# Pooled attention, two heads of a pair on the two halves of the array, in front of two MoE layers

## The chip, the cores and the metric

One Trainium2 chip, one core. The metric is the device time of one execution of the whole kernel in microseconds (us). One profiled execution gives the trace that is read here. Engines: PE is TensorE (PEld its weight loads), DVE VectorE, ACT ScalarE, POOL GpSimd, SP the engine whose queue issues the DMAs.

## What is computed

```python
def attention(q, k, v):              # 4 batches, 8 heads, 1152 keys, head size 64
    q_pool = q.reshape(B, H, S // 2, 2, D).mean(axis=3)          # 576 queries
    scores = scale * q_pool @ k.transpose(0, 1, 3, 2)
    scores = scores - max(scores, axis=-1)
    attn = exp(scores); attn = attn / (sum(attn, axis=-1) + 1e-9)
    return attn @ v
x = attention(q, k, v) as (2304, 512)
h = x @ w_in;   x = (h - tanh(h)) @ w_out            # layer 1, 512 -> 2048 -> 512
h = x @ w2_in;  out = (h * sigmoid(1.702 h)) @ w2_out
```

All in float32. The weights of the two layers come as 8-byte floats.

## The kernel before

A float32 product of full precision is made in one of two ways: as three products in fp32r of a high and a low part (hi·hi, lo·hi, hi·lo), or as one product of plain float32.

**Attention** (L212 to L727) goes over 16 pairs of heads. Keys lie on 128 partitions for two heads: the head size is 64, so one head fills half of the rows. To use all 128 rows, `stack` (L311) builds by six DMAs for each head a stationary array `a1` (high part of k over low part) and `a2` (high part of k over a row of ones), and moving arrays `q2` (high part of q twice) and `q3` (low part of q over the row of minus the maximum). `scores` (L423) makes the scores of one step, 128 keys by 576 queries of one head, in two halves of 288 queries, each from two fp32r products (L433, L434), and takes exp of them on ACT twice: into `pf` (L439) and, for two steps of three, rounded into `ph` (L449). `rest` (L452) makes `pl = pf - ph` on DVE or POOL (L457). A step later `pv` (L459) multiplies by v: for two steps of three six fp32r products (L479), for the third two float32 products (L469). The stationary side is 65 columns wide: v and a column of ones, so row 64 of the result is the sum of the exponentials. There are 18 steps in a pair, nine for each head.

The maximum of every query row is known beforehand: `max_tile` (L322) makes for the next pair a block-diagonal product (`bdqs`, L296) of 128 columns by 288 keys twice (L327) and reduces it on DVE (L331), 18 times for a pair. `max_rows` (L385) transposes the maxima on DVE (L392) and writes them as a row by four DMAs for each head (L400). The first pair has its own opening (L560 to L655): products that only keep PE at work (`keep_warm`, L617), and the maxima of head 0 on 64 rows (`first_max`, L337; L346, L353), with rows made by PE (`row_part`, L360).

A pair's end: `u` takes the result (L485), `sums` (L490) moves the sums by DMA, `recip` (L499), `merge` (L507), `spread` (L513) bring back the reciprocals and `normalise` (L521) writes `xb`.

**What sets the order.** The order of the work on every engine is written out by hand: the loop from L689 issues for each step the scores, the maxima, the rest and the product of three steps before (`LAG`, L538), and the dictionaries `plan`, `opening` and `early` say at which pair and step the preparations of the next pairs run (q sums L283, their split L290 and L294, k's split L303 and L307). `early` also loads seven of the first eight pieces of weights and converts them on DVE (L138, L144, L151, L158), ACT and POOL (L166). Each engine takes its instructions in that order. PSUM has eight banks: two score tiles of two banks, one tile of two for the maxima and two accumulators.

**The two layers** (L729 to L917) follow on the same engines; the last of the eight pieces (`last_o`) is loaded in the attention and converted in the first steps of layer 1. The first product of layer 1 is L755.

Of the kernel before, what the change touches and what calls it, by code (L numbers as in the profile page):

```python
# [7 lines left out]
F32 = mybir.dt.float32  # L8
# [20 lines left out]
def tile_pooled_attention_two_moe(  # L29
# [9 lines left out]
    first: bass.AP,  # L39
# [47 lines left out]
    KG = KT // 3  # L87
    last = 2 * NPAIR - 1
    h0, h1, h2 = last % 3, (last - 1) % 3, (last - 2) % 3
# [8 lines left out]
    a1s, vhs, vls = [{}, {}, {}]  # L98
    for i, at in ((h2, 0), (h1, 3 * S), (h0, 8 * S)):
        a1s[i] = part(at, S)  # L100
        vhs[i] = part(at + S, KT, 128)
        vls[i] = part(at + 2 * S, KT, 128)
    bdqs = [part(6 * S + i * S, S) for i in range(2)]
# [108 lines left out]
    def attention(ctx: ExitStack):  # L212
        ap = ctx.enter_context(tc.tile_pool(name="attn", bufs=1))

        stacks = []
        for i in range(3):
            a1 = a1s[i]
            a2 = ap.tile([D + 1, S], F32R, name=f"a2_{i}")
            q2 = ap.tile([128, SP], F32R, name=f"q2_{i}")
            q3 = ap.tile([D + 1, SP], F32R, name=f"q3_{i}")  # L220
            stacks.append((a1, a2, q2, q3))
        vfs = [rbd[:, SP:SP + KG * 128].rearrange("p (a b) -> p a b", a=KG)] + [
            ap.tile([128, KG, 128], F32, name=f"vf{i}") for i in range(1, 3)]
        vt = [(vhs[i], vls[i]) for i in range(3)]

        def outer(t):
            return t.rearrange("p (m r) d -> p m r d", r=3)[:, :, 0:3:2, 0:D]

        def whole(t):
            return t % 3 == 1  # L230
        nc.vector.memset(f32(bdqs[1][:, 0:128]), 0.0)
        nc.vector.memset(f32(bdqs[1][:, 128:]), 0.0)
        zeros = bdqs[1][:, 0:128], bdqs[1][:, 0:1].to_broadcast([128, 512])

        def refill_v(i, n):
            old, new = [(*vt[x], vfs[x])[n] for x in (0, i)]
            nc.scalar.activation(new[:, :, D:D + 2], old[:, :, D:D + 2], AF.Copy)

        def refill_row(i):
            row = [stacks[x][1][D:D + 1, :] for x in (0, i)]  # L240
            nc.scalar.activation(row[1], row[0], AF.Copy)

        def fill(i):
            vh, vl = vt[i]
            nc.gpsimd.memset(f32(stacks[i][1][D:D + 1, :]), 1.0)
            nc.gpsimd.memset(f32(vh[:, :, D:D + 2]), 1.0)
            nc.gpsimd.memset(f32(vl[:, :, D:D + 2]), 0.0)
            nc.gpsimd.memset(vfs[i][:, :, D:D + 2], 1.0)

        mts = []  # L250
        for i in range(2):
            mt = ap.tile([128, 32], F32R, name=f"mt{i}")
            nc.vector.memset(f32(mt[:]), 0.0)
            mts.append(mt)

        qraw, kraw, vraw, pairs = {}, {}, {}, {}

        def load_q(p, rows=slice(0, 128)):
            if p not in qraw:
                qraw[p] = ap.tile([128, 2, SP], F32, tag="qr", name="qr")  # L260
            nc.sync.dma_start(out=qraw[p][rows], in_=q[p // NPB, p % NPB][rows])

        def load_k(p, rows=slice(0, 128)):
            if p not in kraw:
                kraw[p] = ap.tile([128, S], F32, tag="kr", name="kr", bufs=2)
            nc.sync.dma_start(out=kraw[p][rows], in_=k[p // NPB, p % NPB][rows])

        def load_v(p, s):
            vraw[p, s] = ap.tile([128, 2 * KG, D], F32, tag=f"vr{s}", name=f"vr{s}")
            nc.sync.dma_start(out=vraw[p, s], in_=v[p // NPB, p % NPB][:, s, 0:2 * KG])  # L270

        def new_pair(p):
            pairs[p] = dict(
                qs=ap.tile([128, SP], F32, tag="qs", name="qs"),
                qh=ap.tile([128, SP], F32R, tag="qh", name="qh", bufs=2),
                ql=ap.tile([128, SP], F32R, tag="ql", name="ql", bufs=2),
                kh=ap.tile([128, S], F32R, tag="kh", name="kh", bufs=2),
                kl=ap.tile([128, S], F32R, tag="kl", name="kl"),
                mt=mts[p % 2],
            )  # L280

        def sum_q(p, eng=nc.vector):
            eng.tensor_add(pairs[p]["qs"], qraw[p][:, 0], qraw[p][:, 1])  # L283

        def prep_qs(p, eng=nc.vector):
            new_pair(p)
            sum_q(p, eng)

        def prep_qh(p):
            nc.scalar.activation(pairs[p]["qh"], pairs[p]["qs"], AF.Copy)  # L290

        def prep_ql(p, eng=nc.vector):
            d = pairs[p]
            eng.tensor_tensor(d["ql"], d["qs"], f32(d["qh"][:]), op=ALU.subtract)  # L294

        def prep_bdq(p, s):  # L296
            r = slice(64 * s, 64 * s + 64)
            nc.scalar.activation(
                bdqs[p % 2][r, s * SP:(s + 1) * SP], pairs[p]["qs"][r, :], AF.Copy)

        def prep_kh(p, x):
            xs = slice(x * SP, (x + 1) * SP)
            nc.scalar.activation(pairs[p]["kh"][:, xs], kraw[p][:, xs], AF.Copy)  # L303

        def prep_kl(p, x):
            xs = slice(x * SP, (x + 1) * SP)
            nc.gpsimd.tensor_tensor(  # L307
                pairs[p]["kl"][:, xs], kraw[p][:, xs], f32(pairs[p]["kh"][:, xs]),
                op=ALU.subtract)

        def stack(p, s):  # L311
            d = pairs[p]
            a1, a2, q2, q3 = stacks[(2 * p + s) % 3]
            r = slice(64 * s, 64 * s + 64)
            nc.sync.dma_start(out=f32(a1[0:64, :]), in_=f32(d["kh"][r, :]))
            nc.sync.dma_start(out=f32(q2[0:64, :]), in_=f32(d["qh"][r, :]))
            nc.sync.dma_start(out=f32(a1[64:128, :]), in_=f32(d["kl"][r, :]))
            nc.sync.dma_start(out=f32(q2[64:128, :]), in_=f32(d["qh"][r, :]))
            nc.sync.dma_start(out=f32(a2[0:64, :]), in_=f32(d["kh"][r, :]))
            nc.sync.dma_start(out=f32(q3[0:64, :]), in_=f32(d["ql"][r, :]))  # L320

        def max_tile(p, j, x=0, pool=None, parts=2, n=HB):  # L322
            d = pairs[p]
            mx = (pool or ps_mx).tile([128, parts, 512], F32, tag="mx", name="mx")
            for a in range(parts):
                k0 = (x * parts + a) * n
                nc.tensor.matmul(  # L327
                    mx[:, a, 0:n], bdqs[p % 2][:, 128 * j:128 * j + 128], d["kh"][:, k0:k0 + n],
                    start=True, stop=True)
            c = 16 * x + j  # L330
            nc.vector.tensor_reduce(  # L331
                d["mt"][:, c:c + 1], mx[:, :, 0:n], AX.XY, ALU.max, negate=True)

        ident = bdqs[0][:, 0:128]
        first_mt = bdqs[0][:, 128:288]

        def first_max(s, j, x, pool, parts, n, banks=2):  # L337
            d = pairs[0]
            a1, _, q2, _ = stacks[0]
            r = slice(64 * s, 64 * s + 64)  # L340
            lhs, rhs = (q2, a1) if s == 0 else (d["qh"], d["kh"])
            mx = pool.tile([128, banks, 512], F32, tag="mx", name="mx")
            if j < 4:
                for a in range(parts):
                    k0 = (x * parts + a) * n
                    nc.tensor.matmul(  # L346
                        mx[:, a, 0:n], lhs[r, 128 * j:128 * j + 128], rhs[r, k0:k0 + n],
                        start=True, stop=True)
            else:
                for a in range(parts):  # L350
                    for h in range(2):
                        q0, k0 = 512 + 64 * s - 64 * h, h * SP + a * n
                        nc.tensor.matmul(  # L353
                            mx[:, a, 0:n], bdqs[1][r, q0:q0 + 128], rhs[r, k0:k0 + n],
                            start=(h == 0), stop=(h == 1))
            c = 64 + 16 * x + 5 * s + j
            nc.vector.tensor_reduce(
                first_mt[:, c:c + 1], mx[:, 0:parts, 0:n], AX.XY, ALU.max, negate=True)

        def row_part(s, row, j):  # L360
            c = 5 * s + j
            nc.tensor.matmul(row, first_mt[:, c:c + D + 1], ident, start=True, stop=True)

        def first_row(s, row):
            for j in range(4):
                row_part(s, row[0:D + 1, 128 * j:128 * j + 128], j)

        def copy_row(s, row):
            nc.scalar.activation(stacks[s][3][D:D + 1, 0:512], row[D:D + 1, 0:512], AF.Copy)
# [604 lines left out]
```

## Time and profile before

| | us |
|---|---|
| median of 3 runs | 1302.81 (1298.59 to 1303.04) |
| the profiled execution, its own time | 1298.67 |
| span in its trace, first to last instruction | 1296.0 |
| start of the first product of layer 1 in it | 496.81 |
| mean granted TensorE clock | 0.999 of full |

The span is 2.7 us shorter than the execution's own time. Times in the rows further down are counted from the start of the span. A matmul's record is longer than its share of the engine, since they are pipelined; what one costs is read from the starts of its followers.

### The profile page before, as it was taken

The page shows a single profiled execution, that of the slowest core. Times are in us where ns is not written, and L with a number is a line of the kernel's source. Part 1 is how long each engine was busy: PE and PEld are TensorE (multiplying, and loading weights), DVE is VectorE, ACT ScalarE, POOL GpSimd, SP SyncE. Part 2 cuts the span into 40 slices and gives each one's busy share as a digit, 9 for nine tenths or more (in the row PEclk, how much of TensorE's full clock was granted, in tenths as well). Part 3 has the DMA queues.
Part 4 walks back from the last instruction along what each step waited for, and adds up shares of the span by engine and source line. Part 5 has one row for each costly group of instructions (what it writes and reads, how often), then busy time and mean ns, then how long its engine had stood idle before and what let it go on. Part 6 is the DMA issues. An engine that isn't in the chain of part 4 may idle for free.

```text
span 1296.0 us, 18915 instructions
## 1 busy us (share of the span) xinstructions
PE 1284.7 (99%) x7043; PEld 1134.3 (88%) x7043; DVE 986.5 (76%) x1277; ACT 752.2 (58%) x1159; POOL 358.7 (28%) x277
## 2 busy tenths in 40 slices
PE   9999999999999999999999999999999999999998
PEld 6899999999999988889889889889888889889887
DVE  6787887887978888999999999999944645645433
ACT  6777777777777777786666666666543323222211
POOL 7533333333333332233333333332101100100000
PEclk9999999999999999999999999999999999999999
DMA  7777666676667630211111111111211101111012
GB/s 205 177 176 172 170 157 160 170 184 169 170 168 172 145 96 18 74 33 52 51 40 39 49 33 50 33 33 50 80 34 33 52 30 50 49 33 33 25 41 81
DMA packets 58739, 116.25 MB, mean 90 GB/s; under 512 B 24856, under 2 KB 28952, under 8 KB 58648
## 3 DMA queue, kind: packets, MB, share of 16 engines
q1 hardware_dynamic: 58648, 115.05, 34.1%
q8 instruction: 55, 0.90, 0.3%
q14 instruction: 36, 0.29, 0.1%
HBM read 66.58 MB, written 4.79 MB: 55 GB/s over the span
## 4 chain that ended last, share of the span: by engine, by line
PE 77%; DVE 13%; ACT 6%; issue 2%; POOL 1%; DVEq 0%; POOLq 0%; ACTq 0%
PE y L850 21%; PE h L755 20%; PE pv L479 11%; PE pv L469 7%; PE mx L327 6%; PE sc L434 6%; PE sc L433 6%; DVE gg L813 2%; DVE gg L796 2%; ACT u L794 2%; DVE wt L144 1%; ACT a L815 1%; DVE wt L138 1%; DVE xb L870 1%; DVE wt L151 1%
## 5 line engine op out<-in xcount | busy, mean ns | idle before, releaser
L331 DVE TENSOR_REDUCE mt<-mx 128x1 fp32r<-128x576 f32 x270 | 203.7, 754 | 82.0 <-PE mx L327 76.5
L439 ACT ACTIVATE pf<-sc 128x576 f32<-128x576 f32 x288 | 187.4, 652 | 122.8 <-PE sc L434 112.4
L755 PE MATMUL h<-hl,big 128*128 128x512 f32 (+1 forms) x940 | 211.6, 377 | 0.0
L755 PEld LDWEIGHTS h<-hl,big 128*128 128x128 f32 x940 | 174.0, 188 | 28.5
L850 PE MATMUL y<-g,big 128*128 128x512 f32 (+1 forms) x780 | 185.3, 368 | 1.5 <-POOL g L767 1.5
L433 PE MATMUL sc<-q,big 128*128 128x288 f32 x576 | 182.6, 331 | 0.1
L850 PE MATMUL y<-big,g 128*128 128x512 f32 x702 | 181.0, 390 | 0.0
L166 POOL TENSOR_TENSOR big<-wt,big 128x512 fp32r<-128x512 f32 x46 | 61.3, 1332 | 379.7 <-ACT big L165 379.7
L434 PE MATMUL sc<-q,a 65*128 65x288 f32 x576 | 162.8, 297 | 0.0
L850 PEld LDWEIGHTS y<-g,big 128*128 128x128 f32 x780 | 142.7, 188 | 21.4 <-POOL g L767 3.1
L765 ACT ACTIVATE g<-gg 128x1024 fp32r<-128x1024 f32 (+1 forms) x80 | 78.0, 974 | 138.5 <-DVE gg L826 76.3
L850 PEld LDWEIGHTS y<-big,g 128*128 128x128 f32 x702 | 131.7, 188 | 27.1
L479 PE MATMUL pv<-ph,big 128*65 128x288 f32 x768 | 141.6, 295 | 0.5 <-ACT u L485 0.5
L870 DVE TENSOR_TENSOR xb<-xb,y 128x512 f32<-128x512 f32 (+1 forms) x114 | 72.2, 656 | 86.8 <-PE y L850 86.8
L457 DVE TENSOR_TENSOR pl<-pf,ph 128x576 fp32r<-128x576 f32 x159 | 133.7, 841 | 2.2 <-ACT ph L449 1.5
L755 PE MATMUL h<-hl,w 128*128 128x512 f32 (+1 forms) x564 | 127.0, 377 | 0.0
L449 ACT ACTIVATE ph<-sc 128x576 fp32r<-128x576 f32 x188 | 121.9, 649 | 0.0
L755 PEld LDWEIGHTS h<-hl,w 128*128 128x128 f32 x564 | 104.4, 188 | 17.1
L433 PEld LDWEIGHTS sc<-q,big 128*128 128x128 f32 x576 | 109.4, 190 | 10.8 <-ACT ph L449 0.7
L327 PE MATMUL mx<-kh,big 128*128 128x288 f32 x540 | 117.3, 299 | 1.0 <-DVE mt L331 0.8
L815 ACT ACTIVATE a<-u 128x1024 f32<-128x1024 f32 (+1 forms) x40 | 39.1, 977 | 132.5 <-DVE gg L813 132.4
L434 PEld LDWEIGHTS sc<-q,a 65*128 65x128 f32 x576 | 109.1, 189 | 5.0
(126 smaller groups left out, 2177.7 us busy)
## 6 DMA issues: line engine op xcount, KB each, us to landing
raw<-in_moe_w_in_dram SPq DMA_DIRECT2D x32, 512.0 KB
raw<-in_moe_w_out_dram SPq DMA_DIRECT2D x32, 512.0 KB
big<-kh SPq DMA_DIRECT2D x31, 288.0 KB
q<-qh SPq DMA_DIRECT2D x62, 144.0 KB
big<-kl SPq DMA_DIRECT2D x31, 288.0 KB
a<-kh SPq DMA_DIRECT2D x31, 288.0 KB
kr<-in_k_dram SPq DMA_DIRECT2D x15, 576.0 KB
qr<-in_q_dram SPq DMA_DIRECT2D x15, 576.0 KB
```

The lines of the kernel that those rows point to most:

```text
L327: nc.tensor.matmul(mx[:, a, 0:n], bdqs[p % 2][:, 128 * j:128 * j + 128], d["kh"][:, k0:k0 + n], start=True, stop=True)
L331: nc.vector.tensor_reduce(d["mt"][:, c:c + 1], mx[:, :, 0:n], AX.XY, ALU.max, negate=True)
L433: nc.tensor.matmul(sc[:, x, 0:HB], a1[:, ks], q2[:, xs], start=True, stop=False)
L434: nc.tensor.matmul(sc[:, x, 0:HB], a2[:, ks], q3[:, xs], start=False, stop=True)
L439: nc.scalar.activation(both(pf), sc[:, :, 0:HB], AF.Exp, scale=SCALE)
L449: nc.scalar.activation(both(ph), sc[:, :, 0:HB], AF.Exp, scale=SCALE)
L457: eng.tensor_tensor(pl, pf, f32(ph[:]), op=ALU.subtract)
L469: nc.tensor.matmul(accs[hd][x], vfs[hd % 3][:, t // 3, 0:D + 1], pf[:, x * HB:(x + 1) * HB], start=False, stop=False)
L479: nc.tensor.matmul(accs[hd][x], w[:, t, 0:D + 1], r[:, x * HB:(x + 1) * HB], start=(t == 0 and n == 0), stop=(t == KT - 1 and n == 2))
L755: nc.tensor.matmul(hb[:, j, 0:TBS[b]], wi[:, c, w, :], x[r][c], start=(k == 0), stop=(k == 3 * NKC - 1))
L850: nc.tensor.matmul(ys[m][:, 0:w], lhsT, rhs, start=(fp == 0 and not low and j == p == 0), stop=(fp == 1 and low and j == 1))
L870: nc.vector.tensor_add(dst, dst, ys[m][:, 0:w])
```

## The change

The two heads of a pair are worked on together. Head 0 lies on partitions 0 to 63, head 1 on 64 to 127, and every product of scores or maxima is issued once for each half of the rows, with the same columns; no stacks are built. A step is now 128 keys by 288 queries of both heads (18 steps in a pair as before). The scores take four products for each head: k high · q high, k low · q high, k high · q low, and a row of ones · the row of minus the maximum. exp is taken once. The product with v is plain float32 for all steps, 64 columns wide, head 0 into partitions 0 to 63 of the accumulator and head 1 into 64 to 127, and it is issued in bursts: three steps of scores (with the maxima of the next pair in between), then three products. The sums come from additions of the `pf` tiles: six of the nine on POOL, three on DVE, one addition of the two partial sums on DVE (`merge`), and one float32 product with a matrix of ones (`total`). The maxima take 12 tiles of both heads by 384 keys, and 2 for the last 64 queries of the two heads together. Score tiles and maxima share three PSUM tiles of two banks. All eight pieces of weights are now loaded and converted in the attention, at pairs 3, 4, 6, 7, 9, 10, 12 and 13. New code (removed lines are those of the attention above):

```diff
+        ps = ctx.enter_context(tc.tile_pool(name="ps", bufs=3, space=PSUM))
+        ps_acc = ctx.enter_context(tc.tile_pool(name="ps_acc", bufs=1, space=PSUM))
+        sides = slice(0, 64), slice(64, 128)
...
+        def unit(p, n):
             d = pairs[p]
+            mx = ps.tile([128, 2, 512], F32, tag="ps", name="mx")
+            if n < 12:
+                j, c = divmod(n, 3)
+                for s, r in enumerate(sides):
+                    nc.tensor.matmul(
+                        mx[:, s, 0:KN], d["qh"][r, 128 * j:128 * j + 128],
+                        d["kh"][r, KN * c:KN * c + KN], start=True, stop=True)
...
+            nc.vector.tensor_reduce(
+                d["mt"][:, at:at + 2], mx[:, :, 0:w], AX.X, ALU.max, negate=True)
+        def max_rows(p, part):
...
+            for c in range(n + 2 * part):
...
+                nc.sync.dma_start(
+                    out=row.rearrange("o (a i) -> o a i", i=32),
+                    in_=f32(tt[c:c + 32 * (w // 32 - 1) + 1:32, :]))
+        def scores(g):
...
+            steps = (
+                (d["kh"][:, ks], d["qh"]), (d["kl"][:, ks], d["qh"]),
+                (d["kh"][:, ks], d["ql"]), (sel, d["row"]))
+            for n, (w, m) in enumerate(steps):
+                for s, r in enumerate(sides):
+                    nc.tensor.matmul(
+                        sc[:, s, 0:HB], w[r], m[r, xs], start=(n == 0), stop=(n == 3))
+            pf = ap.tile([128, 2, HB], F32, tag="pf", name="pf", bufs=8)
+            nc.scalar.activation(pf, sc[:, :, 0:HB], AF.Exp, scale=SCALE)
+        def pv(g):
...
+            for s, r in enumerate(sides):
+                nc.tensor.matmul(
+                    accs[p, x][r], pairs[p]["v"][:, s, t, :], probs[g][:, s, :],
+                    start=(t == 0), stop=(t == KT - 1))
+        def add(p, x, who, t, eng=None):
+            eng = eng or (nc.gpsimd, nc.vector)[who]
...
+            eng.tensor_add(out, old, new)
+        def merge(p, x):
+            one, two = parts.pop((p, x, 0))[0], parts[p, x, 1][0]
+            nc.vector.tensor_add(two, two, one)
+        def total(p, x, *more):
...
+                    nc.tensor.matmul(
+                        sm[r], ones, m[:, s, :], start=(n == 0), stop=(n == len(terms) - 1))
+            nc.scalar.activation(results[p][1][:, HB * x:HB * x + HB], sm, AF.Copy)
...
+        for n in range(9):
+            unit(0, n)
+            keep_warm(3)
+        max_rows(0, 0)
+        keep_warm(15)
+        for c in range(NC * NPAIR):
...
+            scores(g)
+            for u in todo[:1]:
+                unit(*u)
+            if part == 0 and before[0] >= 0:
+                merge(*before)
+            scores(g + 1)
+            scores(g + 2)
+            for u in todo[1:]:
+                unit(*u)
+            if c == 4 and p + 1 < NPAIR:
+                max_rows(p + 1, 0)
+            if (p, c) == (0, 1) or p > 0 and c == 0:
+                max_rows(p, 1)
...
+                for t in (0, 1):
+                    add(p, x, 0, 3 * part + t)
+                add(p, x, 1, 3 * part + 2)
+            for i in range(3):
+                pv(g + i)
+            if part == 0 and before[0] >= 0:
+                total(*before)
+            if part == 2:
+                take(p, x)
+            for job in jobs.pop((p, c), ()):
                 job()
```

A pair has six bursts (c = 0 to 5), three for each half of its queries. The jobs at the end of a burst are, among others: k's low part on POOL at c = 0 and 3; q's high part on ACT at 0, its low part on DVE at 2, the sums of q on DVE and `normalise` at 5, k's high part on ACT at 4 and 5. `take` copies the accumulator on ACT at the end of c = 2 and 5. `keep_warm` issues pairs of products of 512 columns.

## Rows read from the trace of the kernel before

**Rows 1.** The page: busy time, share and instructions; engines of the chain that ended last
```profile
PE 1284.7 (99%) x7043; PEld 1134.3 (88%) x7043; DVE 986.5 (76%) x1277; ACT 752.2 (58%) x1159; POOL 358.7 (28%) x277
...
PE 77%; DVE 13%; ACT 6%; issue 2%; POOL 1%; DVEq 0%; POOLq 0%; ACTq 0%
```

**Rows 2.** Busy time by engine in one pair's stretch, then granted clock, DMA share, GB/s
```profile
254.76:284.52 29.76, 29.76 (x206) 27.55 (x205) 26.09 (x41) 22.41 (x41) 10.34 (x10) 1.00 0.74 183
```

**Rows 3.** Timeline of PE inside a pair: start us, length us, line, operation, count
```profile
254.72 1.13 PE L469 MATMUL pv<-pf,rbd 128*65 128x288 f32 x4
...
257.28 0.29 PE L433 MATMUL sc<-q,big 128*128 128x288 f32 x1
...
258.88 0.29 PE L433 MATMUL sc<-q,big 128*128 128x288 f32 x1
...
259.68 1.13 PE L469 MATMUL pv<-pf,rbd 128*65 128x288 f32 x4
260.43 0.51 PE L433 MATMUL sc<-q,big 128*128 128x288 f32 x1
260.78 0.30 PE L434 MATMUL sc<-q,a 65*128 65x288 f32 x1
```

**Rows 4.** Timeline of PE at the start of layer 1
```profile
496.81 4.32 PE L755 MATMUL h<-big,w 128*128 128x384 f32 x24
500.97 4.32 PE L755 MATMUL h<-big 128*128 128x384 f32 x24
```

**Rows 5.** Timeline of PE in the opening
```profile
13.08 0.40 PE L433 MATMUL sc<-q,big 128*128 128x288 f32 x1
...
18.55 0.30 PE L434 MATMUL sc<-q,a 65*128 65x288 f32 x1
18.78 0.79 PE L346 MATMUL mx<-kh,qh 64*128 64x288 f32 x4
19.50 0.48 PE L430 MATMUL sc<-big 128*128 128x512 f32 x1
```

**Rows 6.** Groups by line and shape, ACT
```profile
L439 ACT ACTIVATE pf<-sc 128x576 f32<-128x576 f32 x288 | 187.4, 652 | 122.8 <-PE sc L434 112.4 <-DVE mt L390 10.1
...
L485 ACT ACTIVATE u<-pv 65x288 f32<-65x288 f32 x64 | 22.6, 408 | 1.4 <-PE pv L479 1.4
...
L303 ACT ACTIVATE kh<-kr 128x576 fp32r<-128x576 f32 x30 | 20.4, 680 | 0.4
```

**Rows 7.** Timeline of SP and POOL: DMA issues and what waits for one
```profile
235.47 2.79 SPq L400 DMA_DIRECT2D q<-tt  x4
...
239.50 0.55 SPq L495 DMA_DIRECT2D s<-u  x1
...
241.51 0.20 POOL L502 TENSOR_SCALAR r<-s 128x9 f32<-128x9 f32 x1 [2.23 <-DMA s<-u]
```

**Rows 8.** Groups by line and shape, DVE, until 500 us
```profile
L331 DVE TENSOR_REDUCE mt<-mx 128x1 fp32r<-128x576 f32 x270 | 203.7, 754 | 82.0 <-PE mx L327 76.5
...
L283 DVE TENSOR_TENSOR qs<-qr 128x576 f32<-128x576 f32 x13 | 14.5, 1117 | 0.0
L294 DVE TENSOR_TENSOR ql<-qs,qh 128x576 fp32r<-128x576 f32 x14 | 10.5, 750 | 0.0
...
L357 DVE TENSOR_REDUCE big<-mx 128x1 fp32r<-128x1152 f32 x5 | 6.7, 1358 | 0.9 <-PE mx L346 0.9
...
L144 DVE SCALAR_TENSOR_TENSOR wt<-raw,wt 128x512 int32<-128x512 int32 x8 | 6.3, 786 | 0.0
```

**Rows 9.** Instructions of line 457 on DVE: ns least/median/most
```profile
L457 DVE TENSOR_TENSOR pl<-pf,ph x159: 718/749/1905, 18.4 to 495.2; 128x576 fp32r<-128x576 f32 x159
```

**Rows 10.** Groups by line and shape, POOL; then a stretch of POOL's timeline
```profile
L307 POOL TENSOR_TENSOR kl<-kr,kh 128x576 fp32r<-128x576 f32 x30 | 51.4, 1731 | 0.0
...
20.56 2.79 POOL L307 TENSOR_TENSOR kl<-kr,kh 128x576 fp32r<-128x576 f32 x2
```

**Rows 11.** Groups by line and shape, weight loads
```profile
L434 PEld LDWEIGHTS sc<-q,a 65*128 65x128 f32 x576 | 109.1, 189 | 5.0
...
L469 PEld LDWEIGHTS pv<-pf,vf 128*65 128x65 f32 x252 | 34.2, 137 | 13.3
```

More of the change, by code (lines that the diff above doesn't have):

```diff
@@ L224, in attention @@
[L224 to L237, printed above, removed]
@@ new lines, in attention, with constants @@
+        nil = fixed("nil", 128)
+        sel = ap.tile([128, 128], F32R, name="sel")
+        ones = ap.tile([128, 64], F32, name="ones")
+        mts = [[fixed(f"{nm}{i}", 32) for nm in ("mt", "m2", "m3")] for i in range(2)]
+        corners = [ap.tile([128, 3 * QL], F32R, name=f"cq{i}") for i in range(2)]
+        rows = [ap.tile([128, SP], F32R, name=f"row{i}") for i in range(2)]
+        def constants():
+            nc.gpsimd.memset(f32(sel[:]), 0.0)
+            for r in sides:
+                nc.gpsimd.memset(f32(sel[r.start:r.start + 1, :]), 1.0)
+            nc.gpsimd.memset(ones, 1.0)
+            for t in corners:
+                nc.gpsimd.memset(f32(t[:]), 0.0)
+            for t in rows:
+                nc.gpsimd.memset(f32(t[:]), 0.0)
@@ L259, in load_q, with new, new_pair @@
+        def new(p, nm, n, dt=F32R, bufs=2):
+            pairs[p][nm] = ap.tile([128, n], dt, tag=nm, name=nm, bufs=bufs)
+            return pairs[p][nm]
+        def new_pair(p):
+            mt, m2, m3 = mts[p % 2]
+            pairs[p] = dict(mt=mt, m2=m2, m3=m3, cq=corners[p % 2], row=rows[p % 2])
+        def load_q(p, x=slice(0, SP)):
             if p not in qraw:
                 qraw[p] = ap.tile([128, 2, SP], F32, tag="qr", name="qr")
-            nc.sync.dma_start(out=qraw[p][rows], in_=q[p // NPB, p % NPB][rows])
@@ L322, in max_tile @@
[L322 to L332, printed above, removed]
@@ L360, in row_part @@
[L360 to L369, printed above, removed]
-        def last_copy(s, row):
-            nc.vector.tensor_reduce(
-                stacks[s][3][D:D + 1, 512:SP],
-                row[D:D + 1, :].rearrange("o (h i) -> o i h", h=2), AX.X, ALU.min)
@@ new lines, in load_v, with have, prep_qs, prep_qh @@
+        def load_v(p):
+            pairs[p]["v"] = ap.tile([128, 2, KT, D], F32, tag="v", name="v", bufs=2)
+            nc.sync.dma_start(out=pairs[p]["v"], in_=v[p // NPB, p % NPB])
+        def have(p, nm, *args):
+            return pairs[p].get(nm) or new(p, nm, *args)
+        def prep_qs(p, x=slice(0, SP), eng=nc.vector):
+            qs = have(p, "qs", SP, F32, 1)
+            eng.tensor_add(qs[:, x], qraw[p][:, 0, x], qraw[p][:, 1, x])
+        def prep_qh(p, x=slice(0, SP)):
+            qh = have(p, "qh", SP)
+            nc.scalar.activation(qh[:, x], pairs[p]["qs"][:, x], AF.Copy)
@@ L513, in spread @@
-        def spread(p):
-            d = norm[p]
-            d["rb"] = rbd[:, 0:SP]
-            for s in range(2):
-                r = slice(64 * s, 64 * s + 64)
-                row = d["rd"][r, :].rearrange("p i -> (p i)").unsqueeze(0)
-                nc.sync.dma_start(out=d["rb"][r, 0:SP], in_=row.to_broadcast([64, SP]))
-        def normalise(p, parts=(0, 1)):
-            ua, rb = norm[p]["ua"], norm[p]["rb"]
+            rd = drpool.tile([128, QJ], F32, tag="rd", name="rd", bufs=2)
+            nc.sync.dma_start(out=rd, in_=r9)
@@ L523, in normalise @@
+            norm[p]["rd"] = rd
+        def spread(p):
+            for r in sides:
+                row = norm[p]["rd"][r, :].rearrange("p i -> (p i)").unsqueeze(0)
+                nc.sync.dma_start(out=rbd[r, 0:SP], in_=row.to_broadcast([64, SP]))
+        def normalise(p):
             b, hp = divmod(p, NPB)
-            t0, done, pieces = b * SP, 0, []
+            t0, done = b * SP, 0
             while done < SP:
@@ new lines, in attention @@
+        assert sum(len(u) for u in units.values()) == 14 * NPAIR - 9
+        order = (("i", 0), ("i", 1), ("o", 0), ("i", 2), ("i", 3), ("o", 1), ("o", 2), ("o", 3))
+        for p, (kind, f) in zip((3, 4, 6, 7, 9, 10, 12, 13), order, strict=True):
+            for c, job in enumerate(piece(kind, f)):
+                at(p, c, job)
+        for c in range(NKC):
+            at(NPAIR - 2 + c // 2, 2 * (c % 2) + 1, split_x, 0, [c], nc.gpsimd)
+        for p in range(NPAIR):
+            if p > 0:
+                at(p - 1, 0, load_v, p)
+                at(p - 1, 0, prep_kl, p, 0)
+                at(p - 1, 1, prep_corner, p)
+                at(p - 1, 2, prep_ql, p)
+                at(p - 1, 3, prep_kl, p, 1)
+                at(p, 1, sums, p - 1)
+                at(p, 2, recip, p - 1)
+                at(p, 3, spread, p - 1)
+                at(p, 5, normalise, p - 1)
+            if p > 1:
+                at(p - 2, 3, load_q, p)
+                at(p - 2, 3, load_k, p)
+                at(p - 2, 4, new_pair, p)
+                at(p - 2, 4, prep_kh, p, 0)
+                at(p - 2, 5, prep_kh, p, 1)
+                at(p - 2, 5, prep_qs, p)
+                at(p - 1, 0, prep_qh, p)
@@ new lines, in attention, with keep_warm @@
+        warm = [ps_acc.tile([128, 512], F32, tag=nm, name="warm") for nm in ("acc", "sm")]
+        def keep_warm(n):
+            for _ in range(n):
+                for s, r in enumerate(sides):
+                    nc.tensor.matmul(
+                        warm[s], nil[r], nil[r, 0:1].to_broadcast([64, 512]), start=True, stop=True)
+        early, late = slice(0, 3 * 128), slice(3 * 128, SP)
+        new_pair(0)
+        new_pair(1)
+        load_q(0, early)
+        load_k(0, slice(0, SP))
@@ L953 @@
         laid[name] = x
-    x = _np.asarray(inputs['q'])[0, 0].reshape(s // 2, 2, d).transpose(1, 2, 0)
-    y = _np.asarray(inputs['k'])[0, 0].reshape(2, s // 2, d).transpose(0, 2, 1)
-    laid['first'] = _np.stack([t.reshape(2 * d, s // 2) for t in (x, y)])
     nc = _bacc.Bacc(
```

544 lines of the change are left out of this document (140 added, 404 removed), and 7 rows, old and new, of the table when.

## The prediction

> **What bounds the kernel now.** I read the page first, then a table of busy time by stretch, then timelines of PE. On the page PE is busy for 99% of the span and is 77% of the chain that ended last [rows 1]; the reader should doubt this, since a matmul record is longer than its share. The stretch of one pair shows PE at 29.76 of 29.76 us at full clock, with DVE at 26.1, ACT at 22.4 and POOL at 10.3 us [rows 2]: PE has no gap, and DVE is near behind. The timeline then gives what PE pays. Three steps take 259.68 - 254.72 = 4.96 us, so a pair of 18 steps takes 29.8 us. A step of twelve fp32r products of 288 columns takes 258.88 - 257.28 = 1.60, or 0.133 each. Two float32 products of 288 columns take 260.78 - 259.68 - 0.133 = 0.97, or 0.485 each [rows 3]. Layer 1's first product starts at 496.81, so 16 pairs at 29.8 (476) and some 20 us of opening and end make up the attention; 384 columns cost 4.16 / 24 = 0.173 us [rows 4]. The attention is bound by the columns that stream through PE, and the change cuts these.
>
> **PE after the change, for one pair.** I take it that the two halves of the array stream at the same time, so that two products with 64 rows, or two of 64 columns, cost what one did. No row of before shows two at once; this is the open question of the whole sum, and the rivals price the other answers.
> - Scores: 18 steps of 4 slots, 72 x 0.133 = 9.6 us (as many as now).
> - Maxima: 12 slots of 384 columns at 0.173 and 4 of 288 at 0.133, 2.6 us; now 36 x 0.133 = 4.8.
> - v's product: 18 x 0.485 = 8.7 us; now 12 steps of six at 0.133 and 6 of 0.97, 15.4.
> - Sums: two at 0.485, 1.0 us, new.
> - Changes of the array's shape. A run of four products on 64 rows starts 0.23 us after the last product on 65 rows, 0.10 more than a slot, and the next one on 128 rows starts 0.72 us later where four slots of at most 0.133 are 0.53, so 0.2 goes on leaving [rows 5]. Between scores and v's product every burst changes twice, 0.33 us; six bursts make 2.0 us. Ends: 0.6 (only the cheaper one, each time) and 2.8 (the dearer).
>
> Together 23.9 us in place of 29.8. PE won't run without gaps, though, since the work now comes in bursts through three PSUM tiles:
> - The third score tile of a burst takes the PSUM tile of the first and must wait for its exp of 0.652 us [rows 6]. The first's products end at 0.53 of the burst, its exp some 0.2 later and so at 1.4; PE is done with one tile of maxima and the second of scores at 1.23. About 0.2 lost, 1.2 for six bursts. Ends 0 (the exp starts at once) and 3.
> - ACT takes its work in order. `take` (0.408) can only start when a burst's last product has ended, and at c = 5 a copy of k (0.68) stands behind it [rows 6], ahead of the next exp; at c = 0 the copy of the sums and of q does the same. About 0.35 late each, 0.7. Ends 0 and 1.5.
> - The row of maxima. Six DMAs are issued by SP for `max_rows(p + 1, 0)`; four take 2.79 us to issue, so six take 4.2, and the sums show 1.5 us from the end of an issue (240.05) to their reader (241.51) [rows 7]. The last tile of these maxima comes 2.4 us into c = 4, its reduction and transpose 1.3 later; the row is there at 9.4, and the next pair wants it at 8.9 with bursts of 4.2. About 0.7 lost with the reductions somewhat late. Ends 0 and 2. The second row has three bursts and is hidden by them.
> - DVE. A reduction costs 754 ns for 576 and 1358 for 1152 elements, so 0.955 for 768: 12 of these and 2 of 576 are 13.0 us. Six additions, q's sum and its low part at 0.75 are 6.0; small work (`normalise`, transposes, the reciprocal) 2.5: 21.5 us, of which the page counts a little twice as records overlap. q's sum, issued beside k's low part on POOL, took 1117 where the same shape alone took 750 [rows 8]; ten such operations at 0.37 make 25.2 us. The fullest burst, c = 5, has three reductions, an addition, q's sum and `normalise`, some 6 us against a burst of 4.5, and what is late there holds PE at c = 0. Eight pairs also convert a piece of weights, four operations of some 0.75 [rows 8], so that DVE is full there. I take 0.9 us per pair. Ends 0 and 5, as L457 ranges from 718 to 1905 ns [rows 9].
> - POOL has ten additions and two low parts of k: 12 operations at 1.40 when nothing disturbs (2.79 for two) and 1.73 as the mean [rows 10], 16.8 to 20.8 us. It is hidden by PE's 27 as long as additions aren't late for `merge`, which comes two reductions into the next burst.
>
> Waits 3.5, a pair 27.4 us. What goes at no cost: the six stack DMAs per head (SP), the second exp (18 a pair fewer at most, ACT), the splits of v (POOL); none of them holds PE in [rows 2].
>
> **Opening, end and sum.** Before, the first scores start at 13.08 us [rows 5]. After, products can start at about 5; nine maxima paced by reductions of 0.9 end near 13.0; reduction and transpose 0.5, six issues 4.2, landing 1.5 [rows 7]: the row is there at 19.2. Three of the four products are done by then, so the pairs count from 18.6. The last additions and sums before layer 1: 1.5 us. 18.6 + 16 x 27.4 + 1.5 = 458.5 us against 496.8, that is 38 us less. Layer 1 no longer converts a piece in its first steps; it starts on PE, so I count nothing for it (ends 0 and -3). 1298.7 - 38.3 = 1260.4 us. The profiled execution is 4 us (0.3%) under the median of its three runs; I don't correct for that and say 1260.
>
> **Rivals.**
> - *Weight loads of the two halves don't overlap* (slower). Place: the scores, where every slot now needs two loads of 128 columns. Loads of 128 columns have records of 189 ns and of 65 columns of 137 [rows 11], 0.83 ns per column, so one load streams for about 106 ns. It hides behind 133 ns of columns now; two in a row would take 0.21 us per slot, and the rival decides as soon as they queue. Scores + 5.5, maxima + 0.7, less the 1.2 of waits that then vanish: 32.4 us a pair, 518.4 + 20.1 = 538.5, 42 more than now: 1340. For it: the slope. Against: nothing in the trace; the opening's half-array runs use one half only. The Trainium skill (TensorE: Matmul & The Clock Gate, LDWEIGHTS) states that a load's time goes by its columns and that fewer rows save nothing, about 107 ns for 128 columns as an estimate from its formula; by that alone the halved rows would give this rival's time. Against it the Trainium skill (TensorEngine Tiling (Array Packing), Key Properties) states that different tiles load and multiply in parallel, which would give mine. No row here shows two tiles at once, so I weigh the second higher but leave the rival a real chance.
> - *The halves don't stream together*, so the change doesn't do what it says. If only the column halves of v's product fail: + 9.7, 37.1 us a pair, 1416. If both fail: + 21.9 with all waits gone, 45.8 us, 1555. Nothing in the trace speaks for it or against.
> - *DVE and POOL become the bound.* Two-input operations of both get in each other's way ([rows 8 to 10], 750 against 1117, 1.40 against 1.73, 1905 at most). If each of ten waits for half a POOL operation, 0.7, DVE has 28.5 us, and with four conversions 34.3; with POOL at work seven tenths of the time it is 26.4 and 31.4. Over half the pairs of each kind, PE's 27.4 as floor: 29.4 to 31.4 us a pair, 1293 to 1324; 1305 as its middle. For it: DVE has only 2 us of room in my own sum. Against: L457's median is 749, so most pass unhurt now, with POOL at a third.
>
> **How the numbers follow.** My forecast gets 0.64, DVE and POOL 0.14, weight loads 0.11, streams 0.11. The bounds of the unknown costs inside the forecast go from no waits (23.9, 1204) to waits twice as long (30.9, 1316). The range from 1208 to 1310 holds the forecast and most of the DVE case, about 0.78, and leaves the two costly rivals out. A measurement of this kernel can tell 0.5%, about 6.5 us, from no change. Faster by more: the forecast and a third of the DVE case, 0.69. Within: 0.06. Slower: the rest of it and both costly rivals, 0.25. The likeliest case's own range is 1208 to 1300.
>
> **What would show it.** Right: two half products of the scores start within a few ns of each other or at 0.07 us on average, a pair of v's products every 0.48, a pair takes 26 to 29 us, the granted clock stays at 1.00, and layer 1 starts near 458. Gaps of PE stand before the third score tile and before the fourth product at c = 0. Wrong: scores spaced at 0.1 us each (weight loads) or 0.13 (no overlap); long DVE records over 1.1 us throughout with PE waiting for reductions; a clock at half; or an opening that ends far from 19.

## The result: half a per cent slower, and the profile after

The changed kernel takes 1307.55 us (median of 18 runs, 1303.79 to 1316.28), the kernel before 1299.99 us in the 18 runs beside it (1298.15 to 1304.72). The ratio is 1.0053 with a 95% interval from 1.0037 to 1.0068: slower by 0.5%, where the prediction said 1260 us and faster. The profiled execution took 1308.84 us, with a span of 1307.1 us.

The page of the changed kernel: busy time, share and instructions by engine, then the engines and the lines of the chain that ended last.

```profile
PE 1236.5 (95%) x7950; PEld 984.5 (75%) x7950; DVE 974.4 (75%) x1190; ACT 633.8 (48%) x944; POOL 475.1 (36%) x329
...
PE 52%; DVE 23%; ACT 8%; DMA 8%; issue 5%; SPq 3%; POOL 1%; DVEq 0%; ACTq 0%; POOLq 0%
PE y L670 21%; PE h L575 20%; PE sc L344 4%; PE acc L356 4%; DVE mt L305 4%; DMA kr<-in_k_dram 3%; DVE gg L633 3%; DVE gg L616 2%; SPq L327 2%; DVE s L376 2%; ACT u L614 2%; ACT pf L347 2%; DVE wt L134 2%; ACT a L635 1%; PE mx L292 1%
```

PE's share of the chain falls from 77% to 52% [rows 1]. What takes its place is DVE (23%, before 13%) and two names that were not there at all: DMAs (8%, 3% of them loads of k) and SP's queue (3%, the row DMAs of line 327).

Next, PE's timeline inside a pair, then at the end of the attention (start, length, line, operation, count).

```profile
226.17 0.40 PE L344 MATMUL sc<-qh,kh 64*128 64x288 f32 x2
226.41 0.29 PE L344 MATMUL sc<-qh,kl 64*128 64x288 f32 x2
226.53 0.30 PE L344 MATMUL sc<-ql,kh 64*128 64x288 f32 x2
226.67 0.30 PE L344 MATMUL sc<-row,sel 64*128 64x288 f32 x2
226.80 0.34 PE L292 MATMUL mx<-kh,qh 64*128 64x384 f32 x2
...
229.33 1.68 PE L356 MATMUL acc<-pf,v 128*64 128x288 f32 x12
230.93 0.40 PE L344 MATMUL sc<-qh,kh 64*128 64x288 f32 x2
...
489.01 1.68 PE L356 MATMUL acc<-pf,v 128*64 128x288 f32 x12
492.40 1.68 PE L356 MATMUL acc<-pf,v 128*64 128x288 f32 x12
...
508.46 3.74 PE L575 MATMUL h<-big,w 128*128 128x384 f32 x20
```

Each score line is two half products, and such lines start 0.13 us apart, as a single product did before [rows 3]. Six half products of v, which is three steps, stand as twelve records, two for each float32 product, and take 230.93 - 229.33 = 1.60 us with the change of shape in it. A burst without maxima takes 492.40 - 489.01 = 3.39 us. The work on PE is what was forecast. But layer 1 starts at 508.46 us, 11.7 later than before [rows 4]; behind that point the two kernels take the same (1307.1 - 508.5 = 798.6, and 799 before). So the whole loss lies in the attention, in time in which PE stands still or runs at a lower granted clock (0.992 in the mean of this execution, 0.999 before).

The waits of the first 490 us (engine, line, waited for: us in total, times, longest), without those of engines that nobody waits for:

```profile
PEld sc L344 <- ACT pf L347: 52.8, 77, 3.4
...
PE sc L344 <- ACT pf L347: 30.6, 25, 3.2
...
ACT kh L277 <- DMA kr<-in_k_dram: 23.2, 14, 3.0
ACT wa L127 <- DMA raw<-in_moe_w_in_dram: 15.2, 4, 4.5
PEld mx L300 <- DVE mt L305: 15.2, 14, 1.4
...
ACT wa L127 <- DMA raw<-in_moe_w_out_dram: 12.7, 4, 3.6
```

A wait of PEld, the weight load, and one of PE, the product behind it, are often the same one, so the two aren't to be added. PE waits for exponentials, for up to 3.2 us, while an exponential takes 0.65. ACT for its part waits 23.2 us for k and 27.9 us for weights. A stretch of SP's queue shows where the loads stand:

```profile
290.25 13.02 SPq L327 DMA_DIRECT2D row<-tt  x10
303.32 0.40 SPq L114 DMA_DIRECT2D raw<-in_moe_w_in_dram  x1
```

And ACT's timeline of the same stretch shows what waits for them (idle time before, in brackets):

```profile
291.06 0.69 ACT L277 ACTIVATE kh<-kr 128x576 fp32r<-128x576 f32 x1 [1.81 <-DMA kr<-in_k_dram]
291.65 1.17 ACT L347 ACTIVATE pf<-sc 128x576 f32<-128x576 f32 x2
...
307.01 0.67 ACT L127 ACTIVATE wa<-raw 128x512 f32<-128x512 f32 x1 [2.99 <-DMA raw<-in_moe_w_in_dram]
307.59 0.24 ACT L267 ACTIVATE cq<-qs 128x64 fp32r<-128x64 f32 x1
307.74 1.18 ACT L347 ACTIVATE pf<-sc 128x576 f32<-128x576 f32 x2
```

SP issues a load of weights behind the row DMAs of `max_rows`, six and, two bursts on, four of the same pair, which wait for VectorE's transposes. The load leaves at 303.3; its reader comes one burst later. ACT reaches that read at 304.0, takes its work in order, and stands for 2.99 us with two exponentials behind it; PE's next scores then wait 1.70 us:

```profile
308.42 0.40 PE L344 MATMUL sc<-qh,kh 64*128 64x288 f32 x2 [1.70 <-ACT pf L347]
```

The same happens with k at 291.06. The kernel before asked for such loads much earlier. SP's queue there:

```profile
241.19 0.43 SPq L266 DMA_DIRECT2D kr<-in_k_dram  x1
...
256.86 0.48 SPq L124 DMA_DIRECT2D raw<-in_moe_w_in_dram  x1
```

And ACT's first reads of what the two bring:

```profile
269.59 0.65 ACT L137 ACTIVATE wa<-raw 128x512 f32<-128x512 f32 x1
...
272.71 0.69 ACT L303 ACTIVATE kh<-kr 128x576 fp32r<-128x576 f32 x1
```

There k was issued 31.5 us ahead of its reader (17 steps in the plan) and the weights 12.7 us (six steps), and ACT waited for neither. The change asks for both one burst ahead, which is three steps. So it is the new order of the work that took the lead away, and the shorter pair hardly matters: three steps of the kernel before are 4.96 us [rows 3], and the burst in which ACT waits 2.99 us for the weights takes 4.6.

### The profile page after: what moved, and what is told of

Same layout as the page of the kernel before. It is cut to its first block, busy times and chain, and to the rows that moved or that the text cites. A ratio compares the mean times of both kernels' runs of the same rounds, so it can differ in the third digit from the quotient of the medians.

```text
span 1307.1 us, 20184 instructions
## 1 busy us (share of the span) xinstructions
PE 1236.5 (95%) x7950; PEld 984.5 (75%) x7950; DVE 974.4 (75%) x1190; ACT 633.8 (48%) x944; POOL 475.1 (36%) x329
## 3 DMA queue, kind: packets, MB, share of 16 engines
q8 instruction: 62, 1.02, 0.3%
## 4 chain that ended last, share of the span: by engine, by line
PE 52%; DVE 23%; ACT 8%; DMA 8%; issue 5%; SPq 3%; POOL 1%; DVEq 0%; ACTq 0%; POOLq 0%
PE y L670 21%; PE h L575 20%; PE sc L344 4%; PE acc L356 4%; DVE mt L305 4%; DMA kr<-in_k_dram 3%; DVE gg L633 3%; DVE gg L616 2%; SPq L327 2%; DVE s L376 2%; ACT u L614 2%; ACT pf L347 2%; DVE wt L134 2%; ACT a L635 1%; PE mx L292 1%
## 5 line engine op out<-in xcount | busy, mean ns | idle before, releaser
L305 DVE TENSOR_REDUCE mt<-mx 128x2 fp32r<-128x768 f32 (+1 forms) x224 | 203.4, 923 | 80.2 <-PE mx L292 77.9
L376 POOL TENSOR_TENSOR s<-s,pf 128x576 f32<-128x576 f32 x126 | 179.5, 1425 | 120.2 <-ACT pf L347 115.0
L347 ACT ACTIVATE pf<-sc 128x576 f32<-128x576 f32 x288 | 181.7, 649 | 73.7 <-PE sc L344 70.4
L356 PE MATMUL acc<-pf,v 128*64 128x288 f32 x1152 | 167.4, 428 | 0.0
L344 PE MATMUL sc<-qh,kh 64*128 64x288 f32 x576 | 104.1, 357 | 35.0 <-ACT pf L347 30.6
L344 PEld LDWEIGHTS sc<-qh,kh 64*128 64x128 f32 x576 | 54.6, 185 | 95.3 <-ACT pf L347 52.8
L356 PEld LDWEIGHTS acc<-pf,v 128*64 128x64 f32 x1152 | 76.3, 141 | 61.5 <-issue 23.9
L587 POOL TENSOR_TENSOR g<-gg,g 128x1024 fp32r<-128x1024 f32 (+1 forms) x39 | 87.1, 2234 | 65.2 <-ACT g L585 65.2
L642 ACT ACTIVATE a<-h 128x1024 f32<-128x1024 f32 (+1 forms) x40 | 37.6, 941 | 117.5 <-PE h L575 117.5
L344 PE MATMUL sc<-row,sel 64*128 64x288 f32 x576 | 86.4, 293 | 1.6 <-issue 1.4
```

What stands on the lines that cost most here:

```text
L305: nc.vector.tensor_reduce(d["mt"][:, at:at + 2], mx[:, :, 0:w], AX.X, ALU.max, negate=True)
L344: nc.tensor.matmul(sc[:, s, 0:HB], w[r], m[r, xs], start=(n == 0), stop=(n == 3))
L347: nc.scalar.activation(pf, sc[:, :, 0:HB], AF.Exp, scale=SCALE)
L356: nc.tensor.matmul(accs[p, x][r], pairs[p]["v"][:, s, t, :], probs[g][:, s, :], start=(t == 0), stop=(t == KT - 1))
L376: eng.tensor_add(out, old, new)
L587: eng.tensor_tensor(gt[:, :, 1, :], g, f32(gt[:, :, 0, :]), op=ALU.subtract)
```

## The experiments

Three theories stood against each other. **A**: loads that are asked for one burst ahead arrive too late and hold ACT's queue, and so PE. **B**: two-input additions of VectorE and POOL hold each other up, and PE waits for reductions. **C**: PE's own waits for its PSUM tiles and exponentials make up the rest. Times are medians; ratios are to the kernel before, with their 95% intervals.

**e1, the weights' load five bursts ahead of its conversion, in place of one.**

```diff
 for c, job in enumerate(piece(kind, f)):
-    at(p, c, job)
+    at(*((p - 1, 2) if c == 0 else (p, c)), job)
```

> The load of a piece of weights is issued four bursts earlier (end of c = 2 of the pair before), nothing else. Theory A (late loads): in the eight pairs with a piece ACT waits 3.5 us for it, 27.9 us in all, with every later exp behind it; that wait goes to 0 and the kernel is 20 to 30 us faster than after, about 1280, and the granted clock no longer falls to 0.94 in those stretches. Theory B (DVE and POOL are the bound): DVE is full in these pairs anyway, so its reductions are waited for instead, less than 8 us gained. Theory C (PE's own wait for exp and PSUM tiles): less than 8 us.

1293.97 us, 0.9944 (0.9923 to 0.9964): 13.6 us less than the change.

**e2, the loads of q and k earlier.**

```diff
-    at(p - 2, 3, load_q, p)
-    at(p - 2, 3, load_k, p)
+    at(p - 2, 1, load_q, p)
+    at(*((p - 3, 5) if p > 2 else (0, 0)), load_k, p)
```

> The load of k is issued four bursts earlier and that of q two, nothing else. Theory A: ACT's 23.2 us of waiting for k at c = 4 (1.66 us a pair) go, 10 to 22 us faster than after, about 1290. Theories B and C: less than 5 us.

1301.89 us, 1.0007 (0.999 to 1.0024): 5.7 us less than the change.

**e3, both.**

> Both edits. Theory A: the sum of the two, 35 to 50 us faster than after, 1258 to 1273, which is under before, with plain pairs at 27.4 us as forecast. Theory B: 5 to 15 us, with DVE's reductions as the last thing PE waits for. Theory C: 5 to 15 us, with exp as the last thing.

1285.84 us, 0.9886 (0.9861 to 0.9911): 21.7 us less, near the sum of the two (19.3). Each of the three lies between what theory A and what the other two had said, and in e3 ACT no longer waits for k or weights. Layer 1 starts at 484.60. Late loads alone turn the change from slower into faster. They explain under half of the 47.6 us between 1307.6 and the forecast, so more was needed. The timeline of e3 where one pair passes into the next shows what was left:

```profile
251.50 0.62 ACT L155 ACTIVATE big<-wt 128x512 fp32r<-128x512 f32 x1
...
252.03 0.68 ACT L277 ACTIVATE kh<-kr 128x576 fp32r<-128x576 f32 x1
...
252.55 1.82 DVE L260 TENSOR_TENSOR qs<-qr 128x576 f32<-128x576 f32 x1
252.60 1.18 ACT L347 ACTIVATE pf<-sc 128x576 f32<-128x576 f32 x2
253.29 0.40 PE L344 MATMUL sc<-qh,kh 64*128 64x288 f32 x2 [0.63 <-ACT pf L347]
...
254.30 0.75 DVE L305 TENSOR_REDUCE mt<-mx 128x2 fp32r<-128x576 f32 x1
...
255.10 0.53 PE L300 MATMUL mx<-kh,cq 64*128 64x288 f32 x4 [1.00 <-DVE mt L305]
```

Two lumps: on ACT two copies (0.62 and 0.68) stand ahead of the exponentials that PE waits for, and on VectorE q's addition takes 1.82 us, 0.75 when alone, ahead of the reduction that PE waits for.

**e4, on e3: POOL makes only the first of its five additions in each half of the queries, which leaves four of the nine tiles of `pf` out of the sums.**

```diff
 def add(p, x, who, t, eng=None):
     ...
+    if who == 0 and t > 1:
+        return
```

> As e3_both, and POOL makes only one of its five additions per half pair (four of the nine exponentials are left out of the sums); DVE's own additions stay. Theory B: DVE's two-input operations fall from 1.2 us to about 0.75, some 3 us a pair on DVE, and the kernel is 25 to 50 us faster than e3_both. Theory A: DVE is not what ends last, 0 to 15 us. Theory C: 0 to 5 us.

1270.51 us, 0.977 (0.9731 to 0.981): 15.3 us less than e3, between what theories A and B had said. VectorE's additions of `pf` fall from 1.2 us to 0.75; q's addition, beside which POOL still makes k's low part, stays at 1.21. So B costs something too.

**e5, on e3: all eight additions on POOL, and no merge.**

```diff
-    terms = [parts.pop((p, x, 1))[0], *more]
+    terms = [parts.pop((p, x, 0))[0], *more]
     ...
-    if part == 0 and before[0] >= 0:
-        merge(*before)
     ...
-    for t in (0, 1):
+    for t in range(3):
         add(p, x, 0, 3 * part + t)
-    add(p, x, 1, 3 * part + 2)
```

The last half of the last pair keeps its last two additions on VectorE.

> As e3_both, with all eight additions of a half on POOL and none, nor a merge, on DVE: the sums are complete. DVE loses six two-input operations a pair (7.5 us at the 1.25 us they take), POOL gets six more at 1.41 and is at 26 us of a pair. Theory B in the form that DVE is late: 10 to 25 us faster than e3_both, like e4_few_adds. If POOL's own time is what ends last instead: 0 to 10 us slower than e3_both, with the sums' product waiting for POOL.

1393.36 us, 1.0713 (1.0689 to 1.0738): 107.5 us more than e3. Taking additions from VectorE doesn't take the contention away: the operations that stay there are held longer. Against the second forecast PE does not wait for POOL's sums; it waits 74 us for reductions (24 in e3). Part of that comes from the reciprocal of the sums, whose first operation (L402) stands in POOL's order behind the additions, while VectorE, with reductions behind it, waits for it (waits of e5 until 560 us):

```profile
DVE r L404 <- POOL r L402: 31.0, 14, 3.6
```

In e3 this wait occurs once (1.6 us). The granted clock falls too, to 0.951 in the mean (0.999 in e3); how the 107.5 us divide was not measured. Groups of VectorE in e5, until 560 us (busy, mean ns):

```profile
L271 DVE TENSOR_TENSOR ql<-qs,qh 128x576 fp32r<-128x576 f32 x15 | 28.5, 1900 | 0.0
L260 DVE TENSOR_TENSOR qs<-qr 128x576 f32<-128x576 f32 x14 | 24.5, 1749 | 0.0
L305 DVE TENSOR_REDUCE mt<-mx 128x2 fp32r<-128x576 f32 x30 | 22.5, 751 | 11.4 <-PE mx L300 11.4
```

Both operations stand beside POOL's work and take 1.75 to 1.90 us. The reduction, which reads PSUM and has one input, takes 0.75 as ever.

**e6, on e3: the merge of the two partial sums behind the burst's last reduction, in place of ahead of it.**

```diff
-    if part == 0 and before[0] >= 0:
-        merge(*before)
     scores(g + 1)
     ...
+    if part == 0 and before[0] >= 0:
+        merge(*before)
     if c == 4 and p + 1 < NPAIR:
```

> As e3_both, with the addition of the two partial sums issued on DVE behind the last reduction of its burst in place of ahead of it. If PE loses about 1 us twice a pair because the second maxima tile waits for a reduction that stands behind that addition (32 places, 1 us): 10 to 25 us faster than e3_both. If DVE is late by the sum of its work: 0 to 5 us.

1313.48 us, 1.01 (1.0077 to 1.0123): 27.6 us more than e3. The stall only moved, to the product of the sums, which stands in PE's order ahead of the next scores (waits of e6 until 510 us):

```profile
PEld sm L388 <- DVE s L381: 33.6, 29, 1.9
```

That is 1.2 us each time. Freeing the reductions did not bring it back.

**e7, on e1: the loads of q and k in burst 5 of three pairs ahead, and the preparations of a pair spread over bursts 1, 4 and 5, no two of ACT's copies of k in a row.**

```diff
-    at(p - 2, 3, load_q, p)
-    at(p - 2, 3, load_k, p)
-    at(p - 2, 4, new_pair, p)
-    at(p - 2, 4, prep_kh, p, 0)
-    at(p - 2, 5, prep_kh, p, 1)
-    at(p - 2, 5, prep_qs, p)
-    at(p - 1, 0, prep_qh, p)
+    at(*((p - 3, 5) if p > 2 else (0, 0)), load_q, p)
+    at(*((p - 3, 5) if p > 2 else (0, 0)), load_k, p)
+    at(p - 2, 1, new_pair, p)
+    at(p - 2, 1, prep_kh, p, 0)
+    at(p - 2, 4, prep_kh, p, 1)
+    at(p - 2, 4, prep_qs, p)
+    at(p - 2, 5, prep_qh, p)
```

> As e3_both (loads at the end of c = 5 of the pair before), with q's sum moved from c = 5 to c = 4, k's copies from c = 4 and 5 to 1 and 4, q's copy from c = 0 to 5. ACT no longer has two copies in a row, DVE's fullest burst loses 1.2 us. If these lumps hold PE (0.7 us a pair on ACT by the forecast, 0.5 to 1 on DVE): 10 to 25 us faster than e3_both. If DVE is late by its sum: 0 to 8 us.

1271.97 us, 0.9781 (0.9759 to 0.9803): 13.9 us less than e3, 35.6 less than the change, and the fastest version that computes all of the reference. Nothing of the arithmetic differs from the change. Layer 1 starts at 470.51.

**e8, on e7: the late merge of e6.**

> The moves of e6 and e7 together. If both are places where PE waits: the sum of the two, 20 to 40 us faster than e3_both, about 1250 to 1265, which is what was forecast. If DVE is late by its sum: 0 to 10 us.

1293.26 us, 0.9942 (0.9923 to 0.9962): 21.3 us more than e7, by the same wait (31.1 us, 31 times). The merge belongs where the change has it.

**e9, on e7: the edit of e4.**

> Both loads and the preparations stand as in the spread version (1272.0 us), and POOL makes one addition in each half of the queries; four of the nine tiles of exponentials are left out of the sums. Theory B (VectorE's two-input additions held back by POOL still cost PE time once nothing arrives late): 10 to 16 us less than the spread version, 1256 to 1262, as the same cut gave 15.3 with the preparations in one lump. Rival (the price of the contention was the lump: a held addition only mattered because two bursts' work stood together): within 4 us of the spread version, 1268 to 1274.

1250.57 us, 0.9616 (0.9594 to 0.9637): 21.4 us less than e7, more than theory B had said. Waits of PE's weight loads from 200 to 460 us, in e7:

```profile
PEld sc L344 <- ACT pf L347: 19.9, 52, 0.9
PEld mx L292 <- DVE mt L305: 16.9, 22, 1.1
```

and in e9:

```profile
PEld sc L344 <- ACT pf L347: 19.2, 50, 0.9
...
PEld mx L292 <- DVE mt L305: 5.4, 12, 0.7
```

The wait for reductions shrinks to a third. The wait for the third score tile, theory C, stays and does not depend on POOL.

**e10, on e3: only k's copies moved as in e7; e11, on e3: only q's addition and copy.**

> Both loads early (1285.8 us) and ScalarE's two copies of k moved apart and ahead (bursts 1 and 4 of a pair in place of 4 and 5); q's addition and copy stay where the change has them. Lump on ScalarE (PE waits for an exponential that stands behind a 0.67 us copy): most of the 13.9 us that the spread version gained, 1272 to 1277. Lump on VectorE (q's addition in the last burst holds the maxima of the next one): 1282 to 1288.

> Both loads early (1285.8 us) and only q's addition and its copy one burst ahead; the copies of k stay where the change has them. Lump on VectorE: 1272 to 1278. Lump on ScalarE: 1282 to 1288. If both this and the run with k's copies alone gain about 7, the two lumps share it.

e10: 1290.74 us, 0.9925 (0.99 to 0.9951), 4.9 us more than e3. e11: 1280.22 us, 0.9842 (0.9819 to 0.9866), 5.6 us less. The parts don't add up to e7's 13.9: e10 lies above both forecasts, e11 between them. The lump on VectorE ends last: as long as it is there, relieving ACT gains nothing. A place of e10 shows it:

```profile
164.56 1.91 DVE L421 TENSOR_TENSOR xb<-u,rbd 128x384 f32<-128x384 f32 x2
...
166.40 1.95 DVE L260 TENSOR_TENSOR qs<-qr 128x576 f32<-128x576 f32 x1
...
168.27 0.74 DVE L305 TENSOR_REDUCE mt<-mx 128x2 fp32r<-128x576 f32 x1
...
169.07 0.54 PE L300 MATMUL mx<-kh,cq 64*128 64x288 f32 x4 [2.80 <-DVE mt L305]
```

`normalise` and q's addition hold the reduction until 168.27, and PE stands for 2.80 us. Once q's addition is moved too, the copies of k are worth 8.2 us (e11 against e7, which also loads q earlier). Why e10 is slower than e3 and not equal stays open; four of its 30 us stretches have a granted clock of 0.94 to 0.98, where e3 has one of 0.94.

**e12, on e7: no merge; the product of the sums runs over both partial sums.**

```diff
-    terms = [parts.pop((p, x, 1))[0], *more]
+    terms = [parts.pop((p, x, 0))[0], parts.pop((p, x, 1))[0], *more]
```

> The spread version (1272.0 us) with the addition that joins POOL's and VectorE's partial sums (1.28 us, once in each half) taken out, and the product of the sums run over both partial sums in its place: nothing is left out. PE gets 0.53 us more in each half, 32 x 0.53 = 17 us in the attention. If PE's own work is what bounds a pair now: 1284 to 1290. If VectorE's 1.28 us ahead of the maxima and the wait of the sums' product is worth as much to PE (theory B): 1268 to 1276.

1285.51 us, 0.9884 (0.9863 to 0.9905): 13.5 us more than e7. From its start to the next scores the doubled product takes 1.06 us, the single one in e7 0.59, so 32 of them are some 15 us more and not 17. In e7 work put on PE is paid for nearly in full, and VectorE's 1.2 us per half gives back only some 1.5 us in all.

## Why the prediction was wrong, point by point

- **PE's work, 23.9 us a pair: right.** A burst takes 3.39 us where twelve score slots, three steps of v and two changes of shape were to take 1.60 + 1.45 + 0.33 = 3.38. The open question of the sum, whether two halves stream at once, is answered by the rows at 226 and 229 us.
- **Both costly rivals: out.** Score lines of two products start every 0.13 us, so neither the columns nor the weight loads of the two halves take turns. The Trainium skill (TensorEngine Tiling (Array Packing), Key Properties) states that tiles load and multiply in parallel; the trace agrees.
- **Opening and end: near.** The first product with the row starts at 19.18 us, forecast 19.2. Behind the attention nothing moved, as forecast. The row of maxima, taken at 0.7 us a pair with bursts of 4.2 us (27.4 us a pair make 4.6), costs nothing: behind the opening PE never waits for it.
- **The step that failed: waits of 3.5 us, and so 27.4 us a pair.** With the prediction's own opening and end a pair takes (508.46 - 20.1) / 16 = 30.5 us. The wait for loads had no term at all. The prediction costed what `max_rows` issues on SP only as the path of the row itself (0.7). It didn't ask which loads stand behind those DMAs, nor what stands behind ACT's copies when a load is late. It did not compare the leads either: one burst in the new plan, where the kernel before had 17 steps for k and six for weights. That lead is worth 21.7 us of the 47.6 (e3). The other waits were named but sized too low, as the next points show.
- **ACT's and VectorE's lumps: mechanism right, too small.** The prediction named c = 5 as the fullest burst and c = 0 as the place where PE is held, and took 0.7 us for ACT and 0.9 for VectorE, 1.6 a pair. Spreading the lumps gives back 1.0 us a pair and taking away most of POOL's additions 1.4 more (rows of line 318 below), 2.4 together. ACT's and VectorE's lumps are not terms to be added: e10 and e11 show that the later one hides the other.
- **VectorE against POOL: a rival that was partly true.** The prediction took six additions and q's sum at 0.75 us; they take 1.13 to 1.27 in the changed kernel (below). It counted the extra time as VectorE's busy time, with room for it, though what counts is that a held addition stands ahead of a reduction. On e3 the edit of e4 is worth 15.3 us (at a lower granted clock, last section), on e7 21.4. As the only cause (1293 to 1324) the rival lands on the measured time, but for another reason: without the late loads and the lumps, the same additions on the same engines give 1272, below its range.
- **The third score tile: sized too low.** In e7 PE's weight loads wait 19.9 us for it from 200 to 460 us, at a pair of 28.6 us (next rows) 260 / 28.6 = 9.1 pairs and 2.2 us each, forecast 1.2.
- **The granted clock: not as forecast.** It was to stay at 1.00; in the change six stretches of 30 us show 0.94.
- **The range: luck.** 1307.6 us lies just inside 1208 to 1310. The upper part was there for waits twice as long and for VectorE against POOL; late loads stood in neither.

A small operation that runs once a pair gives the mean of pairs 2 to 14: line 318 (ns least/median/most, first and last start), here in the change.

```profile
L318 DVE TENSOR_TENSOR m<-m x14: 155/156/157, 80.2 to 486.8; 64x2 fp32r<-64x2 f32 x14
```

The same line in e3:

```profile
L318 DVE TENSOR_TENSOR m<-m x14: 155/156/157, 79.0 to 462.9; 64x2 fp32r<-64x2 f32 x14
```

In e7:

```profile
L318 DVE TENSOR_TENSOR m<-m x14: 156/1335/1341, 77.6 to 448.8; 64x2 fp32r<-64x2 f32 x14
```

And in e9:

```profile
L318 DVE TENSOR_TENSOR m<-m x14: 156/1332/1341, 76.6 to 429.7; 64x2 fp32r<-64x2 f32 x14
```

Over 13 pairs that is 31.3 us in the change, 29.5 in e3, 28.6 in e7 and 27.2 in e9. So of the 4.1 us a pair between the change and e9, late loads are 1.8, the lumps 1.0 and POOL's additions 1.4, each with what the clock adds. The forecast's 27.4 is reached only when late loads, lumps and most of POOL's additions are gone: it was the sum of a kernel whose other engines deliver in time.

## What to carry to other kernels

When a change lays the order of the work out anew, compare the leads of the loads before and after, in microseconds: list for each load how long before its first reader it is issued, what stands ahead of it on the issuing queue, when it lands, and what is queued behind that reader. Work for a later stage belongs spread over the bursts, and not ahead of the instruction that frees a buffer on an engine that takes its work in order. Additions split between VectorE and POOL should be costed at their held duration, and judged by what stands behind them, not by the busy share.

## What the runs showed of the hardware

Groups of VectorE in the changed kernel until 500 us, by shape (busy us, mean ns):

```profile
L381 DVE TENSOR_TENSOR s<-s,s 128x576 f32<-128x576 f32 x31 | 39.3, 1267 | 0.0
L376 DVE TENSOR_TENSOR s<-s,pf 128x576 f32<-128x576 f32 x31 | 37.6, 1212 | 2.4 <-ACT pf L347 2.4
...
L305 DVE TENSOR_REDUCE mt<-mx 128x2 fp32r<-128x576 f32 x32 | 23.9, 745 | 1.8 <-PE mx L300 1.8
L260 DVE TENSOR_TENSOR qs<-qr 128x576 f32<-128x576 f32 x14 | 15.8, 1131 | 0.0
```

- With POOL's additions beside them, VectorE's additions with both inputs in SBUF take 1.13 to 1.27 us in the mean, 1.95 in e10's row; with few of POOL's those of `pf` take 0.75 (e4), and in e9 q's addition too. q's low part, a subtraction of this kind, takes 0.70 in the change and 1.90 in e5. The reductions, with one input in PSUM, take the 0.75 they took before [rows 8]. The Trainium skill (SBUF — State Buffer, SBUF: two separate sides) states that such a VectorE operation and a POOL operation that reads SBUF exclude each other for a whole instruction. The means agree with that; no run shows a single lock.
- The granted clock was 1.00 throughout before. In the change six 30 us stretches show 0.94, those of e5, where PE waits most, 0.83 to 0.92 from 80 us on, and all stretches of e7 and e9 between 110 and 440 us 1.00. Gaps alone don't decide: in the change PE is busy for 24.4 of 30 us from 410 us at 1.00, and for 26.9 from 260 us at 0.94. What PE does after a wait can be slower: in e6 PE waits 0.63 and 1.02 us within 2 us, and v's burst at 269.25 then has a record of 3.10 us where the others have 1.68, near the ratio of the levels of 2.4 and 1.2 GHz.
- Over the 18 runs of the change time goes with the mean granted clock: the shortest, 1303.79 us, has 0.995 and the longest, 1316.28 us, 0.985, so 0.001 goes with some 1.2 us (an estimate from the two). By that rate some 8 of the 21.7 us between the change and e3 go with the clock (medians 0.9905 and 0.9975), and e4 (0.993) would have gained some 5 us more at e3's clock, which brings it near e9's 21.4. Which part of a loss the clock causes and which the wait ahead of it was not separated.
